# First expert layer of a transformer block: 256 of its 448 input rows by Strassen's seven block products, with banks of PSUM seeded by other engines

## The chip, the cores and the metric

The kernel runs on one core of a Trainium2 chip. Its engines work side by side, each through its own list of instructions, and wait for each other by semaphores: TensorE (PE in the profile; its weight loads are PEld) multiplies matrices into PSUM, VectorE (DVE), ScalarE (ACT) and GpSimd (POOL) do the element-wise work, and SyncE (SP) issues most DMAs. PSUM has eight banks of 512 float32 columns for each of 128 partitions. The metric is the device time of one execution in microseconds; lower is better.

## What is computed

A parallel block on x of 2048 tokens and 448 features: x plus attention plus a mixture of experts, both on the normalised x.

```python
# A: 16 heads of 28; B: E = 8 experts, K = 8 of them chosen, so all
xn = _layernorm(x, axis=-1)
return x + _A_ref(xn, A_wqkv, A_wo) + _B_ref(xn, B_w_gate, B_w1, B_w2)
...
        for e in range(E):
            mask = (topk_idx == e)
            w = (gates * mask).sum(-1, keepdims=True)
            h = _silu(xf @ w1[e]) @ w2[e]
            out = out + w * h
```

Each expert has a first layer of 448 x 1792 and a second of 1792 x 448. Since eight of eight experts are chosen, every token goes through all of them.

## The kernel before

Precision comes from pairs of float16: each float32 operand is scaled and split in a high and a low part, and a product is three float16 matmuls (high x high, high x low, low x high). In SBUF `xs` holds the normalised x transposed, four row blocks of high and four of low (the fourth block has only 64 rows).

An expert's 1792 hidden columns are cut in 14 blocks of 128, and these in weight groups of 5, 5 and 4 (`GROUPS`), 24 groups in all. The tokens are cut in 4 chunks of 512. `hidden` (L970) makes one hidden block for one chunk: ten matmuls of 128 rows x 512 columns into one bank (L984) and one more on 64 rows only, the tail (L992). Tails use half of TensorE's rows, so two of them, on different row halves and into different banks, are issued side by side; tails of 4 or 6 blocks are gathered (`STAYS`). `silu` (L1022) takes the bank through a tanh (ScalarE), a product (VectorE), a high part (ScalarE) and a low part (GpSimd). `summed` (L1076) makes the second layer for 128 tokens, three matmuls of 448 columns for each block (L1091), which VectorE scales by the gate and adds to `acc` (L1103).

Weights are prepared a group ahead: `load_group` fetches them, `group_scales` finds a power of two, `split_w1` and `split_w2` (L508, L529) scale on ScalarE, take the high part there and the low part on GpSimd. Phase 0 normalises x, transposes it (by DMA for the later chunks) and makes queries, keys and values.

Attention runs beside the experts: a score tile of 128 x 1024 fills the two banks 0 and 1 (L1187), VectorE finds its maxima (L1191), ScalarE takes exponentials (L1207) and their high part (L1215), VectorE the low part (L1210); after transposes by DMA, TensorE weighs the values (L1262, L1269).

The order of all this is not written by hand. Every job is added to a `Plan` (L60) with its engine, an assumed duration, its buffers, what it reads and writes, and a due value `v`; `Plan.run` lists the jobs greedily, for each engine the job of lowest `v` among those that are ready and whose banks are free, and issues the instructions in that order. `Banks.find` (L264) gives out the banks: the pair 0 and 1 to scores, 4, 5, 6, 7, 3 and 2 to all else. On the chip each engine then runs its instructions in the order listed.

## Time and profile before

| | us |
|---|---|
| three runs | 2624.71, 2626.7, 2630.6 |
| median | 2626.7 |
| profiled execution | 2626.05 |
| its span, first to last instruction | 2624.0 |
| TensorE busy | 2610.8 (99%) |
| VectorE busy | 2222.0 (85%) |
| ScalarE busy | 1958.6 (75%) |
| GpSimd busy | 1175.0 (45%) |

An engine's busy time is the union of its instructions' records. A matmul's record runs past the time in which it keeps the next one waiting, so the price of a product is read from start to start in the timeline. Idle time of an engine counts only where the span depends on it.

### The profile page before, as it was taken

What the parts mean: (1) busy time and instruction counts of PE and PEld (TensorE: products, weight loads), DVE (VectorE), ACT (ScalarE), POOL (GpSimd) and SP (SyncE); (2) the same over time, 40 slices, a digit from 0 to 9 for tenths busy, and PEclk for the clock granted to TensorE, in tenths of its full rate; (3) what the DMA queues carried; (4) which work ended last, traced back from release to release, by engine and by line L of the source; (5) the groups of instructions that cost most, each with busy time, mean ns of one, the idle gap of its engine ahead of it and who ended that gap; (6) DMA issues with size and microseconds to landing.
All of it is one profiled execution on the core that took longest, in us unless ns stands there. A gap on an engine that the chain in (4) does not pass through costs nothing.

```text
span 2624.0 us, 46561 instructions
## 1 busy us (share of the span) xinstructions
PE 2610.8 (99%) x17215; PEld 1272.6 (48%) x17215; DVE 2222.0 (85%) x3326; ACT 1958.6 (75%) x2752; POOL 1175.0 (45%) x1081
## 2 busy tenths in 40 slices
PE   9999999999999999999999999999999999999999
...
PEclk9999999999999999999999999999999999999999
...
GB/s 263 167 136 165 157 161 180 161 149 169 162 179 153 167 163 175 166 160 161 173 155 175 150 160 172 157 154 167 162 170 171 149 168 162 146 177 154 156 105 61
DMA packets 1230355, 422.23 MB, mean 161 GB/s; under 512 B 1149232, under 2 KB 1194800, under 8 KB 1230128
## 3 DMA queue, kind: packets, MB, share of 16 engines
...
q14 instruction: 91, 0.75, 0.1%
q10 hardware_dynamic: 560, 0.02, 0.0%
...
## 4 chain that ended last, share of the span: by engine, by line
PE 89%; DVE 6%; ACT 3%; issue 2%; POOL 0%; DMA 0%; DVEq 0%; ACTq 0%; POOLq 0%
PE banks L1091 35%; PE banks L984 34%; PE banks L1187 8%; PE banks L1269 4%; PE banks L1262 2%; PE banks L992 2%; PE banks L835 2%; DVE pl L1210 2%; DVE banks L1191 2%; PE banks L1355 1%; ACT pf L1207 1%; PE banks L858 1%; ACT ph L1215 1%; DVE t L1030 1%; DVE acc L1103 0%
## 5 line engine op out<-in xcount | busy, mean ns | idle before, releaser
L984 PE MATMUL banks<-xs,w 128*128 128x512 f16 x4480 | 1033.6, 379 | 0.8 <-DVE acc L1103 0.5
L1091 PE MATMUL banks<-w,hh 128*128 128x448 f16 x3576 | 968.5, 352 | 1.7 <-DVE acc L1103 1.7
L1034 POOL TENSOR_TENSOR hl<-t,hh 128x512 f16<-128x512 f32 x448 | 601.3, 1352 | 785.9 <-ACT hh L1033 744.5
L1207 ACT ACTIVATE pf<-banks,mx 128x1024 f32<-128x1024 f32 x512 | 568.9, 1111 | 361.0 <-DVE mx L1191 320.5
L1210 DVE SCALAR_TENSOR_TENSOR pl<-pf,ph 128x1024 f16<-128x1024 f32 x512 | 716.9, 1402 | 84.0 <-ACT ph L1215 83.1
L1191 DVE CUSTOM_DVE_ANT_0 banks<-banks,zero,cneg 128x1024 f32<-128x1024 f32 x512 | 657.7, 1285 | 103.4 <-PE banks L1187 78.1
L984 PEld LDWEIGHTS <-w 128*128 128x128 f16 x4480 | 428.5, 97 | 547.3 <-issue 43.2
L1091 PE MATMUL banks<-w,hl 128*128 128x448 f16 x1788 | 629.9, 352 | 0.0
L1215 ACT ACTIVATE ph<-pf 128x1024 f16<-128x1024 f32 x512 | 537.8, 1052 | 5.1
L1091 PEld LDWEIGHTS <-hh 128*128 128x128 f16 x3576 | 347.5, 98 | 348.9 <-issue 8.4
L1027 ACT ACTIVATE t<-banks,the 128x512 f32<-128x512 f32 x448 | 299.4, 683 | 141.3 <-PE banks L992 83.2
L1030 DVE SCALAR_TENSOR_TENSOR t<-t,banks 128x512 f32<-128x512 f32 x448 | 297.2, 679 | 63.7 <-ACT t L1027 62.9
L1103 DVE SCALAR_TENSOR_TENSOR acc<-banks,gwe,acc 128x448 f32<-128x448 f32 x383 | 257.6, 676 | 74.7 <-PE banks L1091 73.5
L1187 PE MATMUL banks<-K,Q 112*128 112x512 f16 x1024 | 305.8, 379 | 3.5 <-ACT pf L1207 3.4
L1033 ACT ACTIVATE hh<-t 128x512 f16<-128x512 f32 x448 | 271.9, 623 | 27.7 <-PE banks L1091 20.5
L522 POOL TENSOR_TENSOR w<-r,w 128x512 f16<-128x512 f32 x112 | 145.8, 1303 | 249.6 <-ACT w L518 243.9
L1091 PEld LDWEIGHTS <-hl 128*128 128x128 f16 x1788 | 174.4, 98 | 163.9
L539 POOL TENSOR_TENSOR w<-r,w 128x448 f16<-128x448 f32 x112 | 127.1, 1137 | 137.3 <-ACT w L536 131.9
L1187 PEld LDWEIGHTS <-Q 112*128 112x128 f16 x1024 | 95.0, 98 | 108.7 <-issue 18.8
L1269 PEld LDWEIGHTS <-th 128*128 128x128 f16 x4096 | 119.2, 96 | 19.7 <-issue 6.4
L387 DVE TENSOR_REDUCE mx<-r 128x1 f32<-128x1280 f32 (+3 forms) x96 | 124.9, 1308 | 0.8 <-DMA r<-in_B_w_dram 0.8
L1269 PE MATMUL banks<-V,th 128*128 128x57 f16 x4096 | 122.3, 188 | 0.0
...
## 6 DMA issues: line engine op xcount, KB each, us to landing
K<-qk SPq DMA_DIRECT2D x512, 56.0 KB
...
Q<-qk SPq DMA_DIRECT2D x256, 28.0 KB
...
```

The costliest lines, as they stand in the source:

```text
L984: nc.tensor.matmul(z(), rows(w)[:, blk, :], xx, start=(i == 0 and not late), stop=(i == NTERM - 2 and late))
L1027: add("ACT", 686, lambda: nc.scalar.activation(t(), z(), AF.Tanh, scale=th_()[:, 0:1]), v, r=[z, th_], w=[t])
L1030: lambda: nc.vector.scalar_tensor_tensor(t(), t(), 1.0, z(), op0=ALU.add, op1=ALU.mult),
L1033: add("ACT", 621, lambda: nc.scalar.activation(hh(), t(), AF.Copy), v, r=[t], w=[hh])
L1034: add("POOL", 1159, lambda: nc.gpsimd.tensor_tensor(hl(), t(), hh(), ALU.subtract), v, r=[t, hh], w=[hl])
L1091: nc.tensor.matmul(y()[:, 0:D], a, wv, start=(i == 0 and u == 0), stop=(i == g - 1 and u == 2))
L1187: nc.tensor.matmul(b()[:, cs], q()[:, q0 : q0 + P], k()[:, cs], start=True, stop=True)
L1191: nc.vector.tensor_tensor_reduce(b(), b(), zero.to_broadcast([P, 2 * C]), cneg, HUGE, op0=ALU.add, op1=ALU.min, accum_out=m()[:, n, j : j ...
L1207: nc.scalar.activation(p(), s(), AF.Exp, bias=m()[:, n, j : j + 1], scale=-1.0)
L1210: nc.vector.scalar_tensor_tensor(l()[:, js], p(), P_SCALE, h()[:, js], op0=ALU.mult, op1=ALU.subtract)
L1215: add("ACT", 1060, lambda: nc.scalar.activation(h()[:, js], p(), AF.Copy, scale=P_SCALE), v, r=[p], w=[(h, j)])
L1269: nc.tensor.matmul(a()[:, n, kt // (NKT // 2), 0:n2], ths[n]()[:, kt], vb()[:, kt, 0:n2], start=(n == 0 and kt == 0), stop=(n == NB - 1 an ...
```

## The change

Two pairs of hidden blocks (0 and 1, 2 and 3 of a group) and one chunk now make a unit. Of the 448 input rows the first two blocks of 128 are taken as a 2 x 2 matrix of blocks: weights A with two row blocks and two hidden blocks, tokens B with two row blocks and two halves of 256 tokens. Strassen's scheme (in Winograd's form) makes the four output blocks from seven products of block sums instead of eight. Each is three float16 matmuls for each of the two pairs, 6 matmuls of 256 columns (`strassen`). Partial sums are shared by seeding: after A11 x B11 in bank b1, ScalarE copies b1 into b2; after S1 x T1 in b3, ScalarE copies b3 to the SBUF tile s5; after S2 x T2 is added in b1, VectorE writes b1 + s5 into b3; after S3 x T3, b1 + s5 into b4. TensorE then goes on accumulating in these banks. The other 192 rows are added as before, 8 matmuls of 256 columns for each output bank (`plain`) and half-height tails, two sets of four in a unit (`tails`). The fifth block of a group of 5 is made by `single`, eleven matmuls of 512 columns, the tail included at full price.

The sums of weights are made in `split_w1` on GpSimd in float32, then split; the sums of x (`sums_of_x`) in phase 0, on VectorE, ScalarE and GpSimd, and transposed by eight more DMAs. The eighth block of `xs` is gone and the sums have a tile `xt` of their own, which phase 0 uses before that for its staging. Banks have kinds (`KINDS`): b1 and b3 come from 3, 2, 7, 6; b2 and b4 from 4 and 5; second-layer sums from 6, 7, 3, 2, 1, 0. High and low parts of the hidden layer have 7 buffers in place of 8, now of 256 tokens for each of two blocks (`columns`); the split weights have three buffers (`wa`) of which a group takes two, and four (`wc`) of which it takes two or three.

The diff, cut to the first layer, the split weights, the sums of x and the loop:

```diff
-RW1, RW2, RH, RPP, RPF = 6, 6, 8, 2, 2
-STAYS = {5: (4, 6, 6, 4), 4: (4, 4, 4, 4)}
+RWA, RWC, RW2, RH, RHC, RT, RPP, RPF = 3, 4, 6, 7, 2, 2, 2, 2
...
+    KINDS = {"s": (0,), "z": (6, 7, 3, 2), "y": (6, 7, 3, 2, 1, 0), "f": (4, 5, 6, 7, 3, 2, 1, 0), "u": (3, 2, 7, 6), "e": (4, 5)}
...
+    W1S = {5: (4, 0, 2), 4: (0, 2)}
+
+    def split_w1(gi, i, v):
+        j = W1S[GROUPS[gi][2]][i]
+        pair = j < 4
+        js = range(j, j + 1 + pair)
...
+        if not pair:
+            add("ACT", 1372, lambda: (scale(), high()), v, r=[so], w=[*keys, (wc, 0)])
+            add("POOL", 1303, low, v, r=[*keys, (wc, 0)], w=[(wc, 1)])
...
+        def highs():
+            scale()
+            for a, h in plain(0):
+                nc.scalar.activation(h, a, AF.Copy)
+
+        def lows():
+            for (a, h), (_, l) in zip(plain(0), plain(1)):
+                nc.gpsimd.tensor_tensor(l, a, h, ALU.subtract)
+            a11, a21, a12, a22 = (r(k, k + 1, f, f + 1) for k in range(2) for f in range(2))
+            nc.gpsimd.tensor_tensor(a22, a21, a22, ALU.add)
+            nc.gpsimd.tensor_tensor(a21, a11, a21, ALU.subtract)
+            nc.gpsimd.tensor_tensor(a11, a22, a11, ALU.subtract)
+            nc.gpsimd.tensor_tensor(a12, a12, a11, ALU.subtract)
...
+        ab = [(r1, j, *k) for j in js for k in R1K[:1]]
+        add("ACT", 2050, highs, v, r=[so], w=[*keys, (wa, 0)])
+        add("POOL", 2500, lows, v, r=[(wa, 0)], w=[*ab, (wa, 1)], steps=6)
+        add("ACT", 630, high, v, r=keys, w=[(wc, 0)])
+        add("POOL", 1303, low, v, r=[*keys, (wc, 0)], w=[(wc, 1)])
+        add("ACT", 630, high_sums, v, r=ab, w=[(wa, 2)])
+        add("POOL", 1303, low_sums, v, r=[*ab, (wa, 2)], w=[(wa, 3)])
...
+            for j in range(2):
+                ns = c * TPC + j, c * TPC + 2 + j
...
+                def sums(xa=xa, ts=ts):
+                    b11, b21, b12, b22 = (xa()[:, i * P : (i + 1) * P] for i in range(4))
+                    t1, t2, t3, t4 = (ts()[:, i * P : (i + 1) * P] for i in range(4))
+                    nc.vector.tensor_tensor(t1, b12, b11, ALU.subtract)
+                    nc.vector.tensor_tensor(t2, b22, t1, ALU.subtract)
+                    nc.vector.tensor_tensor(t3, b22, b12, ALU.subtract)
+                    nc.vector.tensor_tensor(t4, b21, t2, ALU.subtract)
...
+        A11, A12, A22, S2, S3, S4, S1 = range(7)
...
+        def unit(gi, b, tick):
+            ws = [W1[gi, j] for j in (0, 2)]
+            name = f"{gi}_{b}"
+            b1, b3 = (ps_z(f"u{i}{name}", "u") for i in (1, 3))
+            b2, b4 = (ps_z(f"e{i}{name}", "e") for i in (2, 4))
+            s5 = buf("mp", [P, C], F32, f"s5{name}", tag="s5")
...
+            B11, B12, B21, B22 = ((xs[:, k, t[i]], xs[:, 4 + k, t[i]]) for k in range(2) for i in range(2))
+            T1, T2, T3, T4 = ((sums_x[:, i, tx], sums_x[:, 4 + i, tx]) for i in range(4))
+
+            def strassen(bank, slot, x, start=False):
+                def product():
+                    for q in range(2):
+                        h, l = (ws[q][0]()[:, a, slot * P : (slot + 1) * P] for a in range(2))
+                        for i, (w, xx) in enumerate(((h, x[0]), (h, x[1]), (l, x[0]))):
+                            nc.tensor.matmul(
+                                bank()[:, q * HC : (q + 1) * HC], w, xx,
+                                start=(start and q == 0 and i == 0), stop=True, skip_group_check=True,
+                            )
+                keys = [k for w, _ in ws for k in ((w, 0), (w, 1), (w, 2), (w, 3))]
...
+            def plain(bank, f, i):
+                def product():
+                    for q in range(2):
+                        w = ws[q][1]().rearrange("p (a k f c) -> p a k f c", a=2, k=2, f=2)[:, :, :, f]
+                        for ww, xx in (
+                            (w[:, 0, 0], xs[:, 2, t[i]]), (w[:, 0, 0], xs[:, 6, t[i]]), (w[:, 1, 0], xs[:, 2, t[i]]),
+                            (w[:, 0, 1], xs[:, 3, t[i]]),
+                        ):
+                            nc.tensor.matmul(
+                                bank()[:, q * HC : (q + 1) * HC], ww, xx, start=False, stop=True, skip_group_check=True,
+                            )
+                return product, 8 * H_NS, [*xkeys(b), *((w, a) for _, w in ws for a in range(2))]
+
+            def tails(banks_, f):
+                def product():
+                    for q in range(2):
+                        w = ws[q][1]().rearrange("p (a k f c) -> p a k f c", a=2, k=2, f=2)[:, 1, 1, f]
+                        for i, bank in enumerate(banks_):
+                            rs = slice(64 * i, 64 * (i + 1))
+                            nc.tensor.matmul(
+                                bank()[:, q * HC : (q + 1) * HC], w[rs], xs[rs, 3, t[i]],
+                                start=False, stop=True, skip_group_check=True,
+                            )
+                return product, 200 + 2 * H_NS, [*xkeys(b), *((w, a) for _, w in ws for a in range(2))]
...
+            done, v0 = lasty + lastz, at(spent[0]) - AHEAD
+            v = go([b1], strassen(b1, A11, B11, True))
+            add("ACT", 610, lambda: nc.scalar.activation(b2(), b1(), AF.Copy), v, r=[b1], w=[b2])
+            v = go([b3], strassen(b3, S1, T1, True))
+            add("ACT", 610, lambda: nc.scalar.activation(s5(), b3(), AF.Copy), v, r=[b3], w=[s5])
+            tick()
+            v = go([b1], strassen(b1, S2, T2))
+            add("DVE", 690, lambda: nc.vector.tensor_tensor(b3(), b1(), s5(), ALU.add), v, r=[b1, s5], w=[b3])
+            go([b2], strassen(b2, A12, B21), plain(b2, 0, 0))
+            tick()
+            v = go([b1], strassen(b1, S3, T3))
+            add("DVE", 690, lambda: nc.vector.tensor_tensor(b4(), b1(), s5(), ALU.add), v, r=[b1, s5], w=[b4])
+            go([b3], strassen(b3, S4, B22), plain(b3, 0, 1))
+            v = go([b2, b3], tails((b2, b3), 0))
+            silu(gi, b, (0, 0), b2, v)
+            silu(gi, b, (0, 1), b3, v)
+            tick()
+            go([b4], plain(b4, 1, 1))
+            go([b1], strassen(b1, A22, T4), plain(b1, 1, 0))
+            v = go([b1, b4], tails((b1, b4), 1))
+            silu(gi, b, (1, 0), b1, v)
+            silu(gi, b, (1, 1), b4, v)
+            tick()
+
+        def single(gi, b):
...
+                        nc.tensor.matmul(z(), rows[:, blk, :], xx, start=(i == 0), stop=(i == NTERM - 1))
...
+        def columns(gi, b, j, t):
+            if j == 4:
+                return HS[gi, b, 4], slice(t * P, (t + 1) * P)
+            c0 = j // 2 * HC + t % 2 * P
+            return HS[gi, b, (j % 2, t // 2)], slice(c0, c0 + P)
...
```

How the order moves. On TensorE, in weight group 10 (its weights are `w_10_...` before, `wa_...` and `wc_...` now). Before, the tails of four blocks of one chunk stand together between full products:

```order
L1187 MATMUL banks<-K_1_14154,Q_13788 128x512
L992 LDWEIGHTS w_10_1_12809
L992 MATMUL banks<-xs,w_10_1_12809 128x512
L992 LDWEIGHTS w_10_2_13013
L992 MATMUL banks<-xs,w_10_2_13013 128x512
L992 LDWEIGHTS w_10_3_13028
L992 MATMUL banks<-xs,w_10_3_13028 128x512
L992 LDWEIGHTS w_10_4_13051
L992 MATMUL banks<-xs,w_10_4_13051 128x512
L984 LDWEIGHTS w_10_3_13028
```

Now, four tails of one unit stand between a score product and the plain products into b4, whose first waits for VectorE:

```order
L1363 LDWEIGHTS Q_15023
L1363 MATMUL banks<-K_0_15041,Q_15023 128x512
L1132 LDWEIGHTS wc_0_14824
L1132 MATMUL banks<-xs,wc_0_14824 128x256
L1132 LDWEIGHTS wc_0_14824
L1132 MATMUL banks<-xs,wc_0_14824 128x256
L1132 LDWEIGHTS wc_2_14993
L1132 MATMUL banks<-xs,wc_2_14993 128x256
L1132 LDWEIGHTS wc_2_14993
L1132 MATMUL banks<-xs,wc_2_14993 128x256
L1121 LDWEIGHTS wc_0_14824
L1121 MATMUL banks<-xs,wc_0_14824 128x256 [waits DVE_49]
```

The tails have half the columns and come in two such sets a unit; the bank after them is one that VectorE has seeded.

On VectorE, which reads the banks, in group 10, around the silu products of chunk 3 (`t`) before:

```order
L1210 SCALAR_TENSOR_TENSOR pl_14302<-pf_0_14281,ph_14292 128x1024 [waits DMAHW7_49,Activation_49]
L1191 ISA banks,mx_14263<-banks,zero,cneg 128x1024 [waits PE_49]
L1191 ISA mx_14263 128x1
L1030 SCALAR_TENSOR_TENSOR t_1_3_14304<-t_1_3_14304,banks 128x512 [waits Activation_49]
L1030 SCALAR_TENSOR_TENSOR t_2_3_14311<-t_2_3_14311,banks 128x512 [waits Activation_49]
L1287 TENSOR_TENSOR u_14415<-banks,c_14235 128x456 [waits PE_49]
L1191 ISA banks,mx_14263<-banks,zero,cneg 128x1024 [waits PE_49,Activation_49]
L1191 ISA mx_14263 128x1
L1210 SCALAR_TENSOR_TENSOR pl_14302<-pf_1_14339,ph_14292 128x1024 [waits Activation_49]
L1030 SCALAR_TENSOR_TENSOR t_3_3_14452<-t_3_3_14452,banks 128x512 [waits Activation_49]
```

and now, in group 11's first unit, around the two additions (L1151, L1155), with the maximum over scores now on L1367, the eviction of the second layer on L1276 and the low half of the exponentials on L1386:

```order
L1276 SCALAR_TENSOR_TENSOR acc<-banks,gwe_14777,acc 128x448
L1151 TENSOR_TENSOR banks<-banks,s_0_16548 128x512 [waits PE_49,Activation_49]
L1386 SCALAR_TENSOR_TENSOR pl_16517<-pf_1_16520,ph_16494 128x1024 [waits Activation_49]
L1367 ISA banks,mx_16558<-banks,zero,cneg 128x1024 [waits PE_49,Activation_49]
L1367 ISA mx_16558 128x1
L1155 TENSOR_TENSOR banks<-banks,s_0_16548 128x512 [waits DVE_49,PE_49]
L1427 TENSOR_REDUCE top_16627<-mx_16092 128x4
L1428 TENSOR_TENSOR c_16626<-top_16627,mx_16092 128x8 [waits DVE_49]
L1386 SCALAR_TENSOR_TENSOR pl_16631<-pf_0_16582,ph_16594 128x1024 [waits DMAHW6_49,Activation_49]
L1205 SCALAR_TENSOR_TENSOR t_0_00_16643<-t_0_00_16643,banks 128x512 [waits Activation_49]
```

The additions stand among the same maxima, evictions and low halves as the silu products did, and TensorE waits for what they write.

On ScalarE, the last unit of group 10, the copies of b1 and b3 (L1146, L1148) among tanh (L1202), exponential (L1383) and high parts (L1391, L1208):

```order
L1202 ACTIVATE t_3_4_16240<-banks,the_14707 128x512 [waits PE_49,Pool_49]
L1383 ACTIVATE pf_0_16249<-banks,mx_16092 128x1024 [waits DVE_49]
L1146 ACTIVATE banks<-banks 128x512 [waits PE_49]
L1148 ACTIVATE s_3_16261<-banks 128x512 [waits PE_49]
L1391 ACTIVATE ph_16279<-pf_0_16249 128x1024 [waits DMAHW1_49,Activation_49]
L1453 ACTIVATE lt_16285<-banks 128x512 [waits DVE_49,PE_49]
L1208 ACTIVATE hh_3_4_16295<-t_3_4_16240 128x512
L1383 ACTIVATE pf_1_16326<-banks,mx_16092 128x1024 [waits DVE_49]
L1391 ACTIVATE ph_16279<-pf_1_16326 128x1024 [waits Activation_49]
L1383 ACTIVATE pf_0_16358<-banks,mx_16092 128x1024 [waits DVE_49]
L1202 ACTIVATE t_3_00_16373<-banks,the_14707 128x512 [waits PE_49,Pool_49]
L1202 ACTIVATE t_3_01_16378<-banks,the_14707 128x512 [waits PE_49,Pool_49]
```

Both copies stand behind an exponential, and the second right behind the first.

## Rows read from the trace of the kernel before

**Rows 1.** The page: span, then busy time of each engine (share of the span, instructions), then the granted TensorE clock in 40 slices of the span, in tenths, 9 standing for 0.9 or more.
```profile
span 2624.0 us, 46561 instructions
...
PE 2610.8 (99%) x17215; PEld 1272.6 (48%) x17215; DVE 2222.0 (85%) x3326; ACT 1958.6 (75%) x2752; POOL 1175.0 (45%) x1081
...
PEclk9999999999999999999999999999999999999999
```

**Rows 2.** Groups of instructions by line, engine and operation, shapes apart: line, engine, operation, out<-in, partitions x columns, xcount | busy us, mean ns of one | idle us of the engine just before them and who ended it. The first layer's full products and weight loads (L984) and its half-height tails (L992).
```profile
L984 PE MATMUL banks<-xs,w 128*128 128x512 f16 x4480 | 1033.6, 379 | 0.8 <-DVE acc L1103 0.5 <-DVE t L1030 0.2
...
L984 PEld LDWEIGHTS <-w 128*128 128x128 f16 x4480 | 428.5, 97 | 547.3 <-issue 43.2
...
L992 PE MATMUL banks<-xs,w 64*128 64x512 f16 x448 | 66.1, 380 | 0.5 <-ACT lt L1277 0.4
```

**Rows 3.** Timeline of TensorE in a stretch in the middle of the run: start us, us, engine, line, operation, out<-in, xcount. Equal neighbours are merged in one row.
```profile
1003.84 2.32 PE L984 MATMUL banks<-xs,w 128*128 128x512 f16 x10
1006.00 0.60 PE L1187 MATMUL banks<-K,Q 112*128 112x512 f16 x2
1006.43 2.32 PE L984 MATMUL banks<-xs,w 128*128 128x512 f16 x10
1008.69 0.61 PE L992 MATMUL banks<-xs,w 64*128 64x512 f16 x4
1009.23 1.25 PE L984 MATMUL banks<-xs,w 128*128 128x512 f16 x5
1010.32 0.60 PE L1187 MATMUL banks<-K,Q 112*128 112x512 f16 x2
```

**Rows 4.** The table of waits: who waited for whom, us in total, times, longest.
```profile
DVE banks L1191 <- PE banks L1187: 78.1, 72, 3.4
DVE acc L1103 <- PE banks L1091: 73.5, 75, 2.5
...
PE banks L1187 <- ACT pf L1207: 3.4, 5, 1.7
```

**Rows 5.** Busy time in one window, the stage in which experts and attention run together: window, us, then each engine's busy us (instructions), granted clock, DMA share, GB/s.
```profile
150.00:2500.00 2350.00, 2341.98 (x15748) 1143.75 (x15747) 2053.92 (x2992) 1815.16 (x2500) 1096.67 (x1000) 1.00 0.76 162
```

**Rows 6.** Timeline of TensorE at the very end, the closing tile's narrow second-layer products, columns as in rows 3.
```profile
2618.65 0.33 PE L1048 MATMUL banks<-w,hh 128*128 128x192 f16 x2
...
2619.64 0.29 PE L1048 MATMUL banks<-w,hh 128*128 128x144 f16 x2
...
2620.39 0.26 PE L1048 MATMUL banks<-w,hh 128*128 128x112 f16 x2
```

**Rows 7.** Groups by line as in rows 2: on VectorE the low half of a projection taken out of a bank (L844), the maximum over a score tile with its second instruction (L1191), the low half of the exponentials (L1210), a scaling of x (L730), a subtraction of two 128-column tiles (L942); on ScalarE the exponential (L1207), scaling and high half of a first-layer weight block (L517, L518), a copy out of a bank (L842), a 128-column copy (L762); on GpSimd the low half of a weight block (L522).
```profile
L1210 DVE SCALAR_TENSOR_TENSOR pl<-pf,ph 128x1024 f16<-128x1024 f32 x512 | 716.9, 1402 | 84.0 <-ACT ph L1215 83.1
L1191 DVE CUSTOM_DVE_ANT_0 banks<-banks,zero,cneg 128x1024 f32<-128x1024 f32 x512 | 657.7, 1285 | 103.4 <-PE banks L1187 78.1 <-ACT ph L1215 19.2 <-ACT r L535 1.5
...
L1207 ACT ACTIVATE pf<-banks,mx 128x1024 f32<-128x1024 f32 x512 | 568.9, 1111 | 361.0 <-DVE mx L1191 320.5 <-DVE rl L1305 16.2 <-DVE pl L1210 11.0
...
L522 POOL TENSOR_TENSOR w<-r,w 128x512 f16<-128x512 f32 x112 | 145.8, 1303 | 249.6 <-ACT w L518 243.9 <-DMA Q<-qk 3.5
...
L517 ACT ACTIVATE r<-r,scog 128x512 f32<-128x512 f32 x112 | 79.9, 713 | 9.7 <-DVE scog L422 9.6
...
L1191 DVE DVE_READ_ACCUMULATOR2_ANT mx<- 128x1 f32 x512 | 71.2, 139 | 0.0
L518 ACT ACTIVATE w<-r 128x512 f16<-128x512 f32 x112 | 70.5, 630 | 3.5
...
L844 DVE TENSOR_TENSOR ql<-banks,qh 128x512 f16<-128x512 f32 x28 | 19.1, 685 | 16.8 <-ACT qh L842 16.7
...
L842 ACT ACTIVATE qh<-banks 128x512 f16<-128x512 f32 x28 | 16.4, 589 | 23.2 <-PE banks L835 23.1
...
L730 DVE TENSOR_SCALAR xn<-acc,rstd,shift 128x448 f32<-128x448 f32 x12 | 7.1, 628 | 0.0
...
L762 ACT ACTIVATE xb<-xn 128x128 f16<-128x128 f32 x12 | 3.6, 300 | 0.0
...
L942 DVE TENSOR_TENSOR gw<-lg,gm 128x128 f32<-128x128 f32 x1 | 0.3, 294 | 0.0
```

**Rows 8.** Single lines: xcount, ns of one as min/median/max, first and last start us, shape. The low half of the exponentials, an addition of 112 columns on GpSimd, and the transposes of x as SP's queue issues them.
```profile
L1210 DVE SCALAR_TENSOR_TENSOR pl<-pf,ph x512: 1206/1225/4290, 134.8 to 2540.8; 128x1024 f16<-128x1024 f32 x171
...
L1299 POOL TENSOR_TENSOR u<-u x64: 384/390/1453, 182.7 to 2560.4; 128x112 f32<-128x112 f32 x64
...
L772 SPq DMA_TRANSPOSE xs<-xb x12: 1231/1234/2551, 32.1 to 66.9; - x12
```

**Rows 9.** Windows of the opening stage, columns as in rows 5.
```profile
75.00:100.00 25.00, 25.00 (x122) 11.80 (x121) 9.81 (x22) 18.23 (x36) 10.99 (x10) 1.00 0.63 179
100.00:150.00 50.00, 50.00 (x242) 22.55 (x241) 33.55 (x65) 29.91 (x45) 12.83 (x11) 1.00 0.55 147
```

**Rows 10.** Windows between 150 and 2500 us. First the sums over windows of 25 us, chosen by VectorE's busy share: 32 of them below 85%, 21 of 90 to 95%, 8 above 95%. Then a window of 100 us, of those from one full hundred to the next the one with the highest share of VectorE.
```profile
sum 800.00, PE 797.64 PEld 387.69 DVE 650.20 ACT 612.34 POOL 377.23; mean PE 24.93 PEld 12.12 DVE 20.32 ACT 19.14 POOL 11.79
...
sum 525.00, PE 522.37 PEld 256.29 DVE 486.56 ACT 403.22 POOL 223.44; mean PE 24.87 PEld 12.20 DVE 23.17 ACT 19.20 POOL 10.64
...
sum 200.00, PE 198.83 PEld 98.79 DVE 195.21 ACT 152.49 POOL 91.12; mean PE 24.85 PEld 12.35 DVE 24.40 ACT 19.06 POOL 11.39
...
1300.00:1400.00 100.00, 99.75 (x628) 47.49 (x627) 91.61 (x132) 80.59 (x112) 52.09 (x47) 1.00 0.77 173
```

325 lines of the change are left out of this document (182 added, 143 removed).

## The prediction

> **What bounds the kernel now.** I read the page first. TensorE is busy for 2610.8 of 2624.0 us, at the full granted clock in every slice; VectorE for 2222.0, ScalarE for 1958.6, GpSimd for 1175.0 [rows 1]. Busy time of matmuls hides short gaps, since a 512-column matmul is recorded for 379 ns [rows 2] while ten of them take 2.16 us from start to start [rows 3], so I went on to the waits. In the whole table TensorE has one row of note, score products waiting for an exponential: 3.4 us in five waits; VectorE, the other way round, waits 78.1 us for score products and 73.5 us for the second layer's sums [rows 4]. TensorE waits for almost nobody, others wait for it: the span is the sum of its streaming, and a change is worth the columns it takes off TensorE as long as the other engines keep up. How close they are shows in the stage from 150 to 2500 us: in 2350 us TensorE 2341.98 (8.0 idle), VectorE 2053.92 (87.4%), ScalarE 1815.16 (77.2%), GpSimd 1096.67 [rows 5].
>
> **What TensorE saves.** One product's price is a start-to-start time. 512 columns: 2.16 us / 10 = 0.216 us [rows 3]. There are no 256-column ones before, but narrower ones stand at the end: 12 of 192 columns in 2618.65 to 2619.64 us, 82.5 ns each, and 12 of 144 in 0.75 us, 62.5 ns each [rows 6]. That is 0.417 ns a column, so 256 columns take 82.5 + 64 x 0.417 = 109.2 ns, 1.2 ns over half of 0.216. The half-height tails run two at a time; a group of four costs 0.54 us to the next product, and the ten products ahead of it 2.26 instead of 2.16 [rows 3]: beyond two streams of 0.216 a group costs 0.10 + 0.11 = 0.21 us.
> Before: 4480 products [rows 2] x 0.216 = 967.7; 448 tails in pairs, 224 x 0.216 = 48.4; four tail groups for each of 24 weight groups, 96 x 0.21 = 20.2. Sum 1036.3 us.
> After: 24 groups x 4 chunks = 96 units of 7 x 6 + 4 x 8 = 74 products of 256 columns, 96 x 74 x 0.1092 = 775.8; eight half-height tails a unit, in pairs, 96 x 4 x 0.1092 = 41.9; but two tail groups a unit instead of one for four blocks, 192 x 0.21 = 40.3; and the fifth block of 16 groups by itself, 64 x 11 x 0.216 = 152.1. Sum 1010.1 us.
> The saving is 26.2 us, 1.0% of the span. Seven products for eight sound like more: only 256 of 448 rows take part, the tail groups double (20 us), and the single block loses its half-price tail (64 x 0.108 = 7 us). The other products stay.
>
> **What the change adds elsewhere.** (1) VectorE: two additions a unit, a bank plus an SBUF tile into a bank. Nearest row: a bank minus a tile into SBUF, 685 ns; writing a bank shows no surcharge, since the maximum that reads and writes 1024 columns of banks takes 1285 [rows 7]. 192 x 0.685 = 131.5 us. (2) ScalarE: two copies a unit out of a bank, 192 x 0.589 = 113 us [rows 7]. Splitting a pair of weight blocks cost 2 x (713 + 630) = 2.69 us there; now one scaling of 1024 columns (1.11 by the exponential's row), 128 and 256 columns (0.30, and about 0.42 between its neighbours), and 2 x 0.63: 3.09 us, so +0.4 x 48 = 19 us [rows 7]. (3) GpSimd: 2 x 1.303 a pair becomes 2 x 1.303 plus parts of 128 and 256 columns (0.39, about 0.66) and four sums of 128 (0.39 each by the median of a 112-column add [rows 8]): +2.6 us x 48 = 125 us, some 170 if each part of 128 takes the 0.6 mean of that row. All of it is beside TensorE; GpSimd goes to about 52% of its span and has the most room.
> (4) The sums of x, 8 sets: on VectorE two scalings (under 0.63 each) and four sums of 0.294 [rows 7], at most 2.4 us a set, 20 us, late in the opening stage, where VectorE has 9.81 of 25 and 33.55 of 50 us busy [rows 9]: 31 us of room, under TensorE's projection products. Their 8 transposes hold SP's queue 1.23 us each [rows 8], 9.9 us, and the first attention loads stand behind them. If that cover fails, 10 us at most; I take 0, since expert products stand ready. Attention's own pool opens only when phase 0's last buffers have been issued, so its VectorE work may start as much later, and 10 us less of 2324 would raise the share below by 0.4%.
> (5) VectorE also shares with GpSimd: the subtraction of two SBUF tiles has a median of 1225 ns, a longest of 4290 [rows 8] and a mean of 1402 [rows 7], so 512 x 0.177 = 91 us of its busy time is being held up. With 12% more GpSimd work, +11 us.
> The Trainium skill (SBUF — State Buffer, "Who interferes with whom") says that a VectorE instruction with both inputs in SBUF contends with a GpSimd instruction that reads SBUF. The trace agrees so far as that tail reaches; by this rule the new additions, with one input in PSUM, should not be held up.
>
> So VectorE's stage goes from 2053.9 to 2053.9 + 131.5 + 11 = 2196 us, in a stretch of 2350 - 26 = 2324: 94.5%; ScalarE to 1947, 84%. What does TensorE lose then? The same stage holds stretches of such density. In 32 windows with VectorE below 85% (mean 81.3%) TensorE idles 2.36 of 800 us (0.30%); in 21 of 90 to 95%, 2.63 of 525 (0.50%); in 8 above 95% (97.6%), 1.17 of 200 (0.58%) [rows 10]. At 94.5% I take 0.53% of 2324 = 12.3 us against 8.0 now: **+4.3 us**.
>
> **The waits inside a unit.** Banks now go from TensorE to another engine and back. A bank can be read 0.163 us after its last column (379 - 216); a copy is then 0.589. In 15 of 96 units only the six products of S1 (0.66 us) stand between A11 and S2, which refills the copied bank: at least 0.1 us lost each, 1.2 if an exponential (1.11) is just ahead: 1.5 to 18 us. For the additions the order puts at least 14 products, 1.53 us, between S3 and the bank that it seeds, and 12 to 14 between S2 and its users; the addition needs 0.163 + 0.685 = 0.85, so 0.5 to 0.7 is left for what is ahead of it in VectorE's queue, in the order shown a maximum of 1.28 + 0.14 [rows 7] or an eviction. In most units second-layer or score products widen these gaps. Bounds: 0 and two stalls of 0.8 us a unit, 154 us; nearest are the present waits of TensorE, a few us in all, because the written order fills with other ready products. I take **+4 us** for both kinds.
>
> Sum against the profiled execution (2626.05 us, 0.65 below the median of 2626.7): 2626.05 - 26.2 + 4.3 + 4 = 2608, 0.7% less. At the end nothing moves: the closing tile keeps its products.
>
> **Rivals.**
> *VectorE becomes the pace.* For: 94.5% is needed without break, and the best 100 us of the stage reach only 91.6% with TensorE already 0.25 short [rows 10]; scores and evictions hold banks until VectorE has read them, and the units keep four of eight. If 91.6% is all it sustains, the stage takes 2196 / 0.916 = 2397, 47 us longer: 2673, slower. It decides from 93.4% down (2196 / 2350). Against: 25 us windows of 97.6% with TensorE at 99.4%, and VectorE's idle time is mostly spent waiting for TensorE, so it need not be a limit. The Trainium skill (TensorEngine Tiling (Array Packing), "PSUM Bottleneck") warns that a faster TensorE leaves PSUM evacuation as the bottleneck; no row here shows VectorE setting the span yet. Chance 0.16: 0.02 faster, 0.05 same, 0.09 slower.
> *The hand-offs eat it.* Break-even is 26.2 us over 96 units, 0.27 us each. One full wait for a maximum in progress (1.28 us) a unit would be 123 us: 2723. For: VectorE runs its long instructions in the written order. Against: a TensorE with five noted waits now, though every bank of scores and sums already depends on the same engines. Chance 0.13: 0.02 faster, 0.05 same, 0.06 slower.
> *Half-width products cost more than half.* Each carries its own weight load, recorded at 97 ns [rows 2], close to the 109 of the stream. 3.5 ns on each of 96 x 78 would undo the gain. But 144-column products with such loads run at 62.5 ns [rows 6]. Chance 0.03, at or above 2626.
> *Forecast*: 0.68, nearly all faster (0.66; 0.02 same); its own range is 2597 to 2620.
>
> Faster by over 0.2% (below 2621.4) 0.70, within 0.2%, which is what a measurement here can tell from no change, 0.13, slower 0.17. Low end: the full 26 us and some of today's 8 idle gone, 2595. High end: a part of the VectorE case, 93% sustained (2361, +11), or 0.4 us a unit of hand-offs (+12), 2638.
>
> **What would show it.** Right: products of 256 columns 109 ns apart; 192 tail groups at 0.21 us over their stream; VectorE at 93 to 95% between 150 us and the end of attention; TensorE waits from the new additions and copies under 15 us in all; the granted clock at full. Wrong: the additions or ScalarE's copies high in TensorE's waits, VectorE at 97% or more with TensorE idle beside it, later score products, or a gap ahead of each group's first unit, where two sets of split weights must be ready at once with buffers for three.

## The result, and the profile after

The median is 2647.2 us (2645.7 to 2647.7) against 2626.0 for the kernel before in the same comparison: a ratio of 1.0077, interval 1.0059 to 1.0094. The change makes the kernel 0.8% slower; 2608 was forecast, with a range from 2595 to 2638. The profiled execution took 2647.7 us.

The page, for [rows 1]: span, TensorE's busy time, granted clock in 40 slices.

```profile
span 2645.9 us, 54809 instructions
...
PE 2596.9 (98%) x20863; PEld 1597.2 (60%) x20863; DVE 2350.1 (89%) x3567; ACT 2069.8 (78%) x2993; POOL 1356.0 (51%) x1377
...
PEclk9999999999999999999999999999999999999999
```

TensorE has fewer products to stream and is recorded busy 14 us less, but its span is 22 us longer: it stands. The table of waits, for [rows 4], where before had one row of 3.4 us:

```profile
PE banks L1105 <- ACT banks L1146: 14.3, 20, 1.9
PE banks L1363 <- ACT pf L1383: 10.4, 11, 1.8
PE banks L1105 <- DVE banks L1151: 9.9, 11, 1.8
```

TensorE now waits 14.3 us for ScalarE's copy of b1 to b2 (L1146), 9.9 us for VectorE's first addition (L1151), and three times as long as before for exponentials. The window of [rows 5]:

```profile
150.00:2500.00 2350.00, 2310.72 (x19010) 1433.68 (x19009) 2146.63 (x3148) 1905.43 (x2705) 1240.40 (x1247) 1.00 0.77 162
```

39.3 us of TensorE idle in place of 8.0, with VectorE at 91.3% and ScalarE at 81.1%.

A timeline of TensorE shows the products and one of the stands (columns as in [rows 3], with the idle time before a row and its releaser).

```profile
1801.44 0.82 PE L1105 MATMUL banks<-xs,wa 128*128 128x256 f16 x6
1802.09 0.82 PE L1105 MATMUL banks<-xt,wa 128*128 128x256 f16 x6
1802.75 0.60 PE L1363 MATMUL banks<-K,Q 112*128 112x512 f16 x2
1805.22 0.81 PE L1105 MATMUL banks<-xt,wa 128*128 128x256 f16 x6 [1.88 <-ACT banks L1146]
1805.87 0.82 PE L1105 MATMUL banks<-xs,wa 128*128 128x256 f16 x6
1806.53 1.04 PE L1121 MATMUL banks<-xs,wc 128*128 128x256 f16 x8
...
1808.99 1.04 PE L1121 MATMUL banks<-xs,wc 128*128 128x256 f16 x8
1809.96 0.39 PE L1132 MATMUL banks<-xs,wc 64*128 64x256 f16 x4
1810.29 0.60 PE L1363 MATMUL banks<-K,Q 112*128 112x512 f16 x2
```

Read the prices first. Six products of 256 columns take 0.65 us from start to start (1805.22 to 1805.87, 1805.87 to 1806.53 is 0.66), 109 ns each. The four tails and what they cost their neighbours: eight products that alone would be 0.87 us hold the next row for 0.97, and the tails themselves last 0.33 in place of two streams of 0.109; so 0.10 + 0.11 = 0.21. Both are the prediction's numbers. Then the stand: after A11 (1801.44, from `xs`) and S1 (1802.09, from `xt`) comes a score tile, and then TensorE is idle 1.88 us, because S2 (1805.22) may not add to b1 before ScalarE has copied it. ScalarE in the same time:

```profile
1801.45 1.11 ACT L1383 ACTIVATE pf<-banks,mx 128x1024 f32<-128x1024 f32 x1 [3.46 <-DVE rl L1481]
1802.86 0.30 ACT L1487 ACTIVATE ost<-os 128x112 f16<-128x112 f32 x1 [0.30 <-DVE os L1482]
1803.07 1.04 ACT L1391 ACTIVATE ph<-pf 128x1024 f16<-128x1024 f32 x1
1804.01 0.67 ACT L1202 ACTIVATE t<-banks,the 128x512 f32<-128x512 f32 x1
1804.58 0.59 ACT L1146 ACTIVATE banks<-banks 128x512 f32<-128x512 f32 x1
```

A11 is done near 1802.3. The copy (L1146) starts at 1804.58, behind an exponential, a small copy, the exponential's high part and a tanh, in the order as written; TensorE goes on 0.05 us after its end. The waits on copies are mostly of this kind. In the 96 units of the trace only 11 have nothing but S1 between A11 and S2, and these stand 6.3 us in all by the sum below; of the 29 that have a score tile there as well, 17 stand, for 11.2 us.

One sum serves for all that follows. For each product after 110 us I take the time from its start to the next start, less its own pace (columns x 0.417 ns + 2.4 ns, and 0.10 us where products that run side by side, the tails or the attention's L1438, begin or end); what is over 40 ns counts as a **stand**. Recorded idle time is smaller, since a product's record runs on while TensorE already stands. Before has 11.3 us of stands in 27 places, after 60.5 in 118: 19.9 on the copy, 15.0 on the exponentials, 12.8 on the first addition. Profiled time less stands is 2614.8 before and 2587.2 after. So TensorE's own stream fell by 27.6 us, and 49.2 us of stands came for it. (The expectations of w1 and w2 below put the standing at 76 us in after, 25 in before and 33 in w1; by this sum it is 60.5, 11.3 and 24.0.)

### The profile page after: what moved, and what is told of

Its sections match the earlier page's. It is cut to its first block, busy times and chain, and to the rows that moved or that the text cites. A ratio compares the mean times of both kernels' runs of the same rounds, so it can differ in the third digit from the quotient of the medians.

```text
span 2645.9 us, 54809 instructions
## 1 busy us (share of the span) xinstructions
PE 2596.9 (98%) x20863; PEld 1597.2 (60%) x20863; DVE 2350.1 (89%) x3567; ACT 2069.8 (78%) x2993; POOL 1356.0 (51%) x1377
## 4 chain that ended last, share of the span: by engine, by line
PE 54%; DVE 9%; ACT 3%; issue 2%; POOL 1%; DMA 1%; SPq 0%; DVEq 0%; POOLq 0%; ACTq 0%
PE banks L1265 22%; PE banks L1105 10%; PE banks L1121 8%; PE banks L1363 5%; PE banks L1177 3%; DVE banks L1367 3%; PE banks L1445 3%; DVE pl L1386 2%; PE banks L1438 2%; PE banks L1132 1%; DVE t L1205 1%; ACT pf L1383 1%; PE banks L1531 1%; DVE acc L1276 1%; ACT ph L1391 1%
## 5 line engine op out<-in xcount | busy, mean ns | idle before, releaser
L1209 POOL TENSOR_TENSOR hl<-t,hh 128x512 f16<-128x512 f32 x448 | 594.8, 1336 | 810.5 <-ACT hh L1208 753.6
L1383 ACT ACTIVATE pf<-banks,mx 128x1024 f32<-128x1024 f32 x512 | 568.4, 1110 | 287.3 <-DVE mx L1367 248.7
L1386 DVE SCALAR_TENSOR_TENSOR pl<-pf,ph 128x1024 f16<-128x1024 f32 x512 | 719.4, 1407 | 39.7 <-ACT ph L1391 38.7
L1367 DVE CUSTOM_DVE_ANT_0 banks<-banks,zero,cneg 128x1024 f32<-128x1024 f32 x512 | 658.1, 1285 | 69.5 <-PE banks L1363 56.2
L1391 ACT ACTIVATE ph<-pf 128x1024 f16<-128x1024 f32 x512 | 539.0, 1053 | 4.9
L1265 PEld LDWEIGHTS <-hh 128*128 128x128 f16 x3576 | 339.9, 98 | 335.9 <-issue 27.4
L1105 PEld LDWEIGHTS <-wa 128*128 128x128 f16 x4032 | 391.9, 98 | 141.6 <-issue 42.4
L1121 PE MATMUL banks<-xs,wc 128*128 128x256 f16 x3072 | 399.0, 273 | 0.0
L1202 ACT ACTIVATE t<-banks,the 128x512 f32<-128x512 f32 x448 | 298.4, 681 | 101.3 <-POOL hl L1209 50.1
L1105 PE MATMUL banks<-xt,wa 128*128 128x256 f16 x2304 | 313.2, 273 | 26.7 <-ACT banks L1146 14.3
L1121 PEld LDWEIGHTS <-wc 128*128 128x128 f16 x3072 | 294.3, 98 | 62.4 <-issue 15.8
L1363 PE MATMUL banks<-K,Q 112*128 112x512 f16 x1024 | 305.9, 380 | 11.2 <-ACT pf L1383 10.4
L1276 DVE SCALAR_TENSOR_TENSOR acc<-banks,gwe,acc 128x448 f32<-128x448 f32 x383 | 257.2, 677 | 59.0 <-PE banks L1265 58.1
L1208 ACT ACTIVATE hh<-t 128x512 f16<-128x512 f32 x448 | 273.9, 623 | 18.0 <-DVE t L1205 10.2
L1105 PE MATMUL banks<-xs,wa 128*128 128x256 f16 x1728 | 236.5, 273 | 0.0
L611 POOL TENSOR_TENSOR w<-r,w 128x448 f16<-128x448 f32 x112 | 136.5, 1228 | 76.2 <-ACT w L608 74.7
L1177 PE MATMUL banks<-xs,wc 128*128 128x512 f16 x704 | 164.9, 379 | 0.0
```

Of the source, the lines that this page charges most:

```text
L1105: nc.tensor.matmul(bank()[:, q * HC : (q + 1) * HC], w, xx, start=(start and q == 0 and i == 0), stop=True, skip_group_check=True,)
L1121: nc.tensor.matmul(bank()[:, q * HC : (q + 1) * HC], ww, xx, start=False, stop=True, skip_group_check=True,)
L1202: add("ACT", 686, lambda: nc.scalar.activation(t(), z(), AF.Tanh, scale=th_()[:, 0:1]), v, r=[z, th_], w=[t])
L1209: add("POOL", 1159, lambda: nc.gpsimd.tensor_tensor(hl(), t(), hh(), ALU.subtract), v, r=[t, hh], w=[hl])
L1265: nc.tensor.matmul(y()[:, 0:D], a, wv, start=(i == 0 and u == 0), stop=(i == g - 1 and u == 2))
L1276: lambda: nc.vector.scalar_tensor_tensor(acc[:, n, :], y()[:, 0:D], gb()[:, n : n + 1], acc[:, n, :], op0=ALU.mult, op1=ALU.add),
```

## The experiments

A reply, below, is a copy or addition on another engine that TensorE's next step in a unit needs. The expectations set four theories against each other. Density: the added work on VectorE and ScalarE makes every reply late. Hand-off: TensorE loses the whole of each wait for a reply. Half-width: the narrow products stream slower than reckoned. Written order: TensorE stands because nothing else is ready at that moment.

Ratios are to the kernel before, timed beside each. "Rest" is the profiled time less the stands; it tells whether the stands are all that differs.

| run | median us | ratio, interval | stands us | rest us |
|---|---|---|---|---|
| d1, before with the load at any time | 2690.0 | 1.0243, 1.0228 to 1.0258 | 57.7 | 2632.8 |
| d2, before with the load in its place | 2624.7 | 0.9996, 0.9987 to 1.0005 | 10.7 | 2613.9 |
| b1, before with the rule | 2621.8 | 0.9987, 0.9977 to 0.9996 | 8.3 | 2613.5 |
| o1, as o3 but additions with both inputs in SBUF | 2662.8 | 1.0140, 1.0125 to 1.0155 | 75.0 | 2586.8 |
| o2, copies free, order of after | 2643.1 | 1.0064, 1.0047 to 1.0081 | 57.7 | 2586.5 |
| o3, copies and additions free, order of after | 2638.5 | 1.0047, 1.0032 to 1.0063 | 52.7 | 2586.2 |
| x1, as o3, planned anew | 2650.5 | 1.0097, 1.0082 to 1.0112 | 63.5 | 2586.9 |
| e1, x1 with shifted attention | 2627.2 | 1.0008, 0.9998 to 1.0018 | 39.6 | 2587.5 |
| e2, after with shifted attention | 2644.4 | 1.0071, 1.0055 to 1.0087 | 59.1 | 2588.9 |
| w1, other order | 2611.2 | 0.9945, 0.9932 to 0.9957 | 24.0 | 2588.4 |
| a1, w1 without overlap | 2641.8 | 1.0060, 1.0043 to 1.0077 | 54.0 | 2587.6 |
| a2, after with overlap | 2619.2 | 0.9975, 0.9964 to 0.9985 | 32.6 | 2586.6 |
| w2, better order | 2601.8 | 0.9912, 0.9897 to 0.9927 | 14.9 | 2587.4 |
| a3, w2 with the rule | 2626.8 | 1.0005, 0.9995 to 1.0015 | 40.8 | 2587.2 |
| n1, w2 with copies and additions free | 2602.4 | 0.9915, 0.9898 to 0.9933 | 14.0 | 2588.0 |

Apart from d1, which lost time before 110 us, where this sum does not count, the rest is 2613.5 to 2614.8 for every kernel with eight products and 2586 to 2589 for every one with seven, in whatever order. What differs from run to run is the stands. In a few runs they hold something besides waits: products at the lower granted clock behind a long stand, which are over their pace though nothing holds them up. They make some 13 us of x1's stands, 9 of e2's, 7 of d1's, 3 to 5 of a1's, a3's and e1's, and under 2 of any other run's.

**Is it the load on the other engines?** My first try, d1, let the extra work start at any time.

```diff
+ if j < 2:   add("ACT", 610, <copy of a constant to scratch>, v)
+ elif j < 4: add("DVE", 690, <addition of constants to scratch>, v)
```

> The kernel before with the load of the change and none of its hand-offs: for every expert slice and quarter of the tokens two more ScalarE copies (512 columns) and two more VectorE additions (512 columns), 192 of each in all, which write a scratch tile that nobody reads; the order is planned anew with them in it. What the reference asks is still computed. Density theory: this alone gives the loss, 2640 us and more, with the score products (L992 in before) standing 10 us longer on the exponentials than the 4.8 us of before. Hand-off theory: the load alone costs under 8 us, 2627 to 2634 us, and TensorE's standing grows by no more than that. My term for it in the prediction was 4.3 us, 2630 us.

(The score products of before are L1187; L992 are the tails.) It took 2690.0 us, far above every theory's figure. The windows show why: the work stood ready from the start, ScalarE was busy 56.2 of the first 60 us (35.9 before) and TensorE 48.5 (57.7 before), and the setup came late. All of the work was done by 657 us. As a measure of the density of after it is void, but while the work lasts it shows a higher one:

```profile
300.00:700.00 400.00, 381.88 (x2527) 184.02 (x2524) 390.10 (x560) 294.89 (x404) 186.21 (x161) 0.99 0.71 154
```

VectorE is busy 97.5% of these 400 us, and TensorE idles 18.1 (1.7 in before). d2 ties the same work to the blocks:

```diff
+ if j < 2:   add("ACT", 610, lambda: nc.scalar.activation(idle_a, z(), AF.Copy), v, r=[z])
+ elif j < 4: add("DVE", 690, lambda: nc.vector.tensor_tensor(idle_d, z(), <0>, ALU.add), v, r=[z])
```

> The kernel before with the load of the change, this time in its place: behind the tanh's bank of every first to fourth hidden block, one more reader of that bank, a ScalarE copy (two blocks of the four) or a VectorE addition (the other two) of 512 columns into a scratch tile that nobody reads, 192 of each in all; TensorE waits for none of them except as the bank comes free 0.6 to 0.7 us later. What the reference asks is still computed. In the run d1 the same work could start at any time, was done in the first quarter of the span, and held up the attention's setup (TensorE busy 48.5 of the first 60 us against 57.7 in before), so it did not measure density. Density theory: 2640 us or more, as after. My prediction's term for density was 4.3 us: 2630 us. Written-order theory (the load fits as long as other products stand ready whenever TensorE waits for a reply): under 5 us, 2626 to 2631 us.

No difference from before. The window of d2:

```profile
150.00:2500.00 2350.00, 2345.05 (x15695) 1143.62 (x15694) 2129.92 (x3134) 1880.56 (x2660) 1102.37 (x995) 1.00 0.74 160
```

VectorE at 90.6% and ScalarE at 80.0%, near after's 91.3 and 81.1, and TensorE idle 5.0 us. At this density the added load of the two engines costs nothing; the density theory falls. (GpSimd's added work is not in d2, 1102 us in the window against 1240 in after; w2 below has it all and is faster than before.)

**Is it the replies themselves?** The next runs keep every engine's order of after and take away the readers of b1 that TensorE waits for. The copy of b3 into s5 and the writes into the second banks stay.

```diff
- lambda: nc.scalar.activation(b2(), b1(), AF.Copy)
+ lambda: nc.scalar.activation(b2(), <0>, AF.Copy)             # o1, o2, o3
- lambda: nc.vector.tensor_tensor(b3(), b1(), s5(), ALU.add)   # and b4
+ lambda: nc.vector.tensor_tensor(b3(), <0>, s5(), ALU.add)    # o1
+ lambda: nc.vector.tensor_tensor(b3(), b3(), s5(), ALU.add)   # o3
```

> The kernel after with the order of every engine kept row for row, but the ScalarE copy into the second bank and the two VectorE additions take a constant zero in place of the first bank, so TensorE waits for them only where it goes on in the bank that they fill, and no longer before its next product in the first bank. The part of the sum that they carried over is left out, so the hidden layer is another one. Hand-off theory (the loss is TensorE standing before its next product until ScalarE or VectorE has read the bank): the trace of after has 19.9 us of standing before L1105 on the copy (33 times) and 12.8 us on the additions (18 times); both go, so about 2647 - 33 = 2614 us. Density theory (131 us more VectorE work and 113 us more ScalarE work make every reply late, whoever asks): the work is all still there, so within 5 us of after, 2642 to 2650 us, with the standing moved to the score products and the second bank. Half-width theory (the narrow products and the half-height pairs stream slower than reckoned): unchanged, 2645 to 2649 us.

o1 was slower still: 2662.8 us (1.0140, 1.0125 to 1.0155). Its additions, with both inputs in SBUF, first as o1 has it, then as after has it, with one input in PSUM (min/median/max):

```profile
L1155 DVE TENSOR_TENSOR banks<-zero,s x96: 683/727/1651, 127.6 to 2632.7; 128x512 f32<-128x512 f32 x96
```

```profile
L1155 DVE TENSOR_TENSOR banks<-banks,s x96: 679/699/736, 127.4 to 2621.3; 128x512 f32<-128x512 f32 x96
```

Some now last 1.65 us, and VectorE is busy 46 us longer. The Trainium skill (SBUF — State Buffer, "Who interferes with whom") says that such an instruction contends with GpSimd's reads of SBUF; the pair of rows agrees. So o1 measured a new cost of its own making, and o3 repeats it without.

> As the run before it, but only the ScalarE copy takes the constant; the two additions read the first bank as in after. The carried-over part is left out of the second bank alone. Hand-off theory: the 19.9 us on the copy go and the 12.8 us on the additions stay: about 2627 us, and the run without either hand-off lies some 13 us below this one. Density theory: 2642 to 2650 us. If the copy is late only because TensorE came early (so that the time is lost a step later whatever it is that waits), the standing before the additions and before the score products grows by as much as the copy's goes, and the time is that of after.

> As o1 (order of after kept row for row, no reader of the first bank between its products), but each addition reads the PSUM bank that it writes in place of a constant in SBUF: in o1 the additions had both inputs in SBUF and took up to 1.67 us (median 0.73), and VectorE was busy 46 us longer than in after, a cost of its own. The carried-over part is again left out, so the hidden layer is another one. Hand-off theory: 2647 - 33 = 2614 us. Late-engine theory (in this order ScalarE and VectorE are behind at these places, so whatever TensorE reaches next waits as long; o2, which cut the copies alone, took 16 us off the waits at the copies and got 4 us): 2635 to 2645 us, with the standing before score products and second banks grown.

o2 got 4 us of the 19.9 that stood on the copy, and o3 8.7 of the 32.7 on copy and addition. The waits of o3:

```profile
PE banks L1363 <- ACT pf L1383: 16.4, 26, 1.9
PE banks L1105 <- DVE banks L1151: 4.6, 6, 1.2
PE banks L1105 <- ACT banks L1146: 4.1, 7, 1.2
```

The stands on copy and addition fell from 32.7 to 11.6 us (those left are first products in a bank that the reply fills), and those on exponentials grew from 15.0 to 25.3. In a fixed order a wait that is taken out mostly comes back at the next thing that is late. The hand-off theory, that each wait is worth its length, falls too.

**Is it the order?** w1 has all instructions, shapes and hand-offs of after.

```diff
-RWA, RWC, RW2, RH, RHC, RT, RPP, RPF = 3, 4, 6, 7, 2, 2, 2, 2
+RWA, RWC, RW2, RH, RHC, RT, RPP, RPF = 3, 3, 6, 7, 2, 3, 2, 2
...
-            done, v0 = lasty + lastz, at(spent[0]) - AHEAD
+            done, v0 = [], at(spent[0]) - AHEAD
-            v = go([b1], strassen(b1, A11, B11, True))
+            v = go([b1], strassen(b1, A11, B11, True), early=20, free=0)
...
+            v = go([b3], strassen(b3, S1, T1, True), early=60, free=0)
...
```

`done` is the rule: the last second-layer job and single block in the list, for which every product of a unit waits. The lines left out put the copy 20 and the additions 50 ahead, move the calls of `tick` (the steps of a unit at which second-layer groups are handed out), let the splitting of weights begin two of these steps later and, at the end of the file, change offsets between attention and experts.

> The kernel after with the same instructions, shapes and hand-offs, in another written order: a unit no longer has to wait until the second-layer products ahead of it are issued, its first two products are offered 20 and 60 us earlier so that their copies are made while TensorE has the unit before in hand, copies and additions are put ahead of other replies by 20 and 50 us, second-layer groups are handed out at other steps of the unit, and one buffer of the split weights is given up for a third of the tanh. Written-order theory (TensorE stands because at those moments nothing else is ready): the streams of after without standing are 2646 - 76 = 2570 us, and with as much standing as the kernel before has (25 us) that is a span of 2595, some 2597 us of time; 2595 to 2615 us. Density theory (VectorE busy 91% and ScalarE 81% of the middle stage make replies late in any order): 2635 to 2650 us. Hand-off theory (a reply takes so long that a unit can't be worked without a wait of 0.34 us): 2635 to 2650 us.

2611.2 us, 36 us under after and 0.55% under before. Which of the edits?

> The order of w1 (2611.2 us) with one thing taken back: a unit again waits until the second-layer products ahead of it are issued, its first two products are offered no earlier than the rest, and copies and additions are not put ahead. The other edits of w1 (third tanh buffer for one of the split weights, other steps for the second-layer groups, other offsets of the two streams of work) stay. If it is the overlap of a unit's start with the work ahead that takes TensorE's standing away: 2635 to 2650 us, with the standing before L1105 on the copy back at 10 us or more. If the order is only another draw among many and any edit moves it: anywhere from 2611 to 2650 us, with no reason for the standing to come back at the copy.

> The other way round: after with the overlap of w1 (a unit need not wait for the second-layer products, first two products offered 20 and 60 us earlier, copies and additions ahead by 20 and 50 us), the third tanh buffer and the other steps for the second-layer groups, but with all offsets between the attention's and the experts' work as in after. If the overlap carries w1's gain of 36 us, most of it is here too: 2612 to 2628 us. If the offsets carry it: 2635 us or more.

Both came out as the overlap has it: without it 2641.8, with it and the old offsets (and the old first step of the splitting) 2619.2. In a1 11.1 us of stands are back on the copy, 1.9 in w1. w2 is a shorter edit found along that line (the single block is free of the rule too). It also moves the offsets, `M_AT, A_AT, LEAD` from 60, 0, 130 to 57, 45, 70, which its expectation does not name.

> A shorter edit of the order than w1 and one that I think better: no unit and no single block waits for the second-layer products, the first two products of a unit are offered 20 and 10 us earlier, the additions are put ahead by 50 us, the third tanh buffer, second-layer groups handed out later in the unit. Instructions, shapes and hand-offs are those of after. By the written-order theory its floor is the span without standing of after and w1 (2646 - 76 = 2570 us; 2611 - 33 = 2578 us); with a third to a half of w1's 33 us of standing it comes to 2590 to 2605 us, under w1 and under both kernels of the case. Density theory: not under w1's 2611 us.

2601.8 us, 0.88% under before and 45 us under after; 14.9 us of stands. Its two longest rows of waits, and its window:

```profile
PE banks L1363 <- ACT pf L1383: 2.5, 4, 1.3
PE banks L1438 <- DMA tl<-pl: 2.3, 3, 1.4
```

```profile
150.00:2500.00 2350.00, 2340.51 (x19280) 1459.10 (x19279) 2162.87 (x3180) 1920.62 (x2741) 1263.55 (x1276) 1.00 0.76 163
```

No copy or addition is left at the top, and VectorE is at 92.0%, more than in after. TensorE's timeline about a unit's start shows what changed:

```profile
1169.31 0.82 PE L1105 MATMUL banks<-xs,wa 128*128 128x256 f16 x6
...
1172.80 0.60 PE L1363 MATMUL banks<-K,Q 112*128 112x512 f16 x2
1173.23 0.82 PE L1105 MATMUL banks<-xt,wa 128*128 128x256 f16 x6
...
1177.16 2.54 PE L1177 MATMUL banks<-xs,wc 128*128 128x512 f16 x11
1179.54 0.82 PE L1105 MATMUL banks<-xt,wa 128*128 128x256 f16 x6
```

A11 at 1169.31, S1 at 1173.23, S2 at 1179.54, with second-layer products, score tiles and the single block between. ScalarE's copy lies well inside:

```profile
1170.66 0.59 ACT L1146 ACTIVATE banks<-banks 128x512 f32<-128x512 f32 x1
```

Between the end of A11 and S2, after had S1 and a score tile, 1.1 us, for the reply to come; w2 has 9.6.

**The rule, the replies, or both?**

```diff
-            done, v0 = [], at(spent[0]) - AHEAD
+            done, v0 = lasty + lastz, at(spent[0]) - AHEAD       # w2 to a3; and after=lasty in single
```

> The order of w2 (2601.8 us) with the rule alone put back: a unit, and the single block of a five-slice group, again wait until the second-layer products ahead of them are issued; the earlier offer, the additions' 50 us, the third tanh buffer and the later hand-out stay. If the rule is what leaves TensorE without other work while a reply is out: a good part of the 45 us between after and w2 comes back, 2615 to 2640 us, with the standing before score products and L1105 up from 15 us to 30 or more. If any of the other edits did it: within 5 us of w2, 2597 to 2607 us.

The rule alone costs w2 25 us. The waits of a3:

```profile
PE banks L1363 <- ACT pf L1383: 8.8, 10, 2.7
PE banks L1105 <- ACT banks L1146: 6.4, 14, 0.8
PE banks L1105 <- DVE banks L1151: 3.7, 6, 1.0
```

> The kernel before with the rule of after: no hidden block starts until the second-layer products handed out ahead of it are issued. Its blocks need no reply between their products. If the rule alone costs the time, hand-offs or not: 2640 us or more. If it needs both, units that wait for replies inside and a rule that keeps other units out: 2622 to 2630 us, as before.

On before, the same rule costs nothing (it came out 4 us faster). Its blocks have no reply inside; that this is the reason is argued, since a block of eleven products differs from a unit in more than that. The converse, the rule without the first bank's replies, planned anew:

> The kernel after, rule and units as they are, with the first bank's readers taken away as in o3 (copy of a constant, additions that read the bank they write; the carried-over part is left out, so the hidden layer is another one), but with the order written anew for it: in o3 the order was still the one written for units that wait. If hand-offs need both (rule and replies), the standing should fall well below the 53 us of o3: 2590 to 2615 us. If the rule on a long serial unit is enough even without replies: 2630 to 2642 us.

This did not fit: 2650.5. TensorE's timeline at one of its stands, then GpSimd's, then three windows:

```profile
1047.20 2.54 PE L1177 MATMUL banks<-xs,wc 128*128 128x512 f16 x11
1050.24 0.59 PE L1363 MATMUL banks<-K,Q 112*128 112x512 f16 x2 [0.50 <-ACT pf L1383]
1053.88 1.01 PE L1363 MATMUL banks<-K,Q 112*128 112x512 f16 x2 [3.04 <-ACT pf L1383]
1058.21 1.01 PE L1363 MATMUL banks<-K,Q 112*128 112x512 f16 x2 [3.32 <-ACT pf L1383]
1059.01 1.49 PE L1105 MATMUL banks<-xs,wa 128*128 128x256 f16 x6
1060.29 2.55 PE L1105 MATMUL banks<-xt,wa 128*128 128x256 f16 x12
```

```profile
1056.56 2.13 POOL L590 TENSOR_TENSOR wa<-r,wa 128x512 f16<-128x512 f32 x1
1058.65 2.02 POOL L611 TENSOR_TENSOR w<-r,w 128x448 f16<-128x448 f32 x2
```

```profile
1030.00:1045.00 15.00, 15.00 (x158) 8.67 (x156) 14.14 (x30) 13.10 (x18) 6.29 (x10) 1.00 0.75 172
1045.00:1060.00 15.00, 8.13 (x35) 3.59 (x33) 12.90 (x18) 14.26 (x22) 14.27 (x16) 0.74 0.74 165
1060.00:1075.00 15.00, 14.80 (x115) 9.72 (x114) 13.18 (x19) 11.82 (x17) 7.19 (x5) 0.92 0.86 172
```

TensorE has three score tiles in 9 us, each waiting for an exponential. GpSimd splits the next weights until 1058.69 (L590), and the first products of the unit that uses them start at 1059.01, six of them in 1.28 us in place of 0.65 at the lower clock. The like happens near 1685, 2024 and 2330 us, 6 to 7 us each time. I read this as the experts' work running ahead of its weights, so that the order had only score tiles to offer; the trace itself shows TensorE waiting for exponentials alone. Two numbers hold the attention back against it:

```diff
-M_AT, A_AT, LEAD, END, LAND, TURN = 60.0, 0.0, 130.0, 2585.0, 3500, 4500
+M_AT, A_AT, LEAD, END, LAND, TURN = 60.0, 45.0, 80.0, 2585.0, 3500, 4500
```

> x1 (rule kept, the first bank's readers taken away, order written anew, 2650.5 us) with the attention's work set 45 us later against the experts' at the start and 50 us later at the end, two numbers of the order. In x1 the standing came in heaps of some 7 us at the start of an expert (1050 to 1059 us: three score products and nothing else, until GpSimd had the next slice's split weight ready 0.3 us before the first product that uses it). If x1 was slow because the experts' work ran ahead of its weights and not because of the rule: 2605 to 2625 us, with the heaps gone. If the rule with a serial unit is enough to cost the time: 2640 us or more.

> The kernel after, readers of the first bank and all, with the same two numbers (45 us later at the start, 50 us at the end). With e1 it gives the price of the replies under the rule: if the replies are the cause under the rule, this stays at 2635 to 2650 us while e1 falls to 2605 to 2625. If the two numbers alone mend it, 2605 to 2625 us here as well.

e1 is at 2627.2, 23 us under x1 and 2 us above its forecast; one heap of 11 us (1349 to 1371 us) and one of 4 are left. e2 stays at 2644.4. With the rule and these offsets the first bank's replies cost 17 us, some 5 of them as products at the lower clock. They are not all of it: e1, with the rule and without them, still has 39.6 us of stands, 17.6 of them on exponentials.

> w2 (2601.8 us) with its order kept row for row and the first bank's readers taken away as in o3 (the carried-over part is left out). If the replies themselves cost nothing once other work stands between a product and the one that needs its reply: 2599 to 2603 us, as w2, where the same cut in the order of after gave 8.7 us. If each unit still pays for them: 2590 us or less.

2602.4 against 2601.8: where other work stands between, the first bank's replies cost nothing that can be measured. Against e1, n1 lacks the rule and has w2's other edits, and its stands are 14.0 in place of 39.6. The replies left in the unit, the copy of b3 and the fills of the second banks, were not taken out in any run.

## Why the prediction was wrong

- **The stream: right.** 26.2 us were forecast, from 109.2 ns a product and 0.21 us a tail group; the rest of the profiled time fell by 27.6, and the timeline has both prices. "Half-width products cost more than half" is out.
- **Density, +4.3 us: a small step, and too much.** VectorE was put at 94.5% of the stage and reached 91.3%: the stage grew longer instead of shorter (the last low half of an exponential starts at 2559.9 us, 2540.8 in [rows 8]), and the 11 us of hold-up by GpSimd did not come (that instruction has a mean of 1407 ns, 1402 in [rows 7]). d2 puts the price of the load at nothing. "VectorE becomes the pace" is out at this density: w2 runs at 92.0% in 2601.8. At 97.5%, in d1, TensorE does stand.
- **"I take +4 us for both kinds": this step failed.** Stands grew by 49 us, 0.51 us a unit, where break-even was 0.27: 33 us on the copy and the first addition, 10 more at the score tiles. "The hand-offs eat it" is what happened, though its price was 123 us and the wait it named, behind VectorE's long instructions, was the smaller part: 12.8 us on the addition, 19.9 on ScalarE's copy.
- **Why the step failed.** I priced the case of S1 alone between A11 and S2 at 1.5 to 18 us, and it came to 6.3 (11 units in the trace; I had counted 15). I took a score product between them for cover, and lost 11.2 us there: in the stand shown the copy waited behind an exponential, a small copy, a high part and a tanh, where I had reckoned with one exponential at most, and TensorE lost 2.0 us by the sum of starts (my most was 1.2). Then I chose near 0 "because the written order fills with other ready products". That was read off the kernel before, whose ready products were other hidden blocks, free to run in any bank. The change takes just these away: a unit is one chain, and `done` keeps the next unit out until the second-layer products are issued. Cover that an order has today was counted as cover for a change that removes it.
- The gap ahead of a group's first unit, which I named as a sign of error, is seldom in after (2.0 us near 1067, at a score tile); x1 has it four times in full.

Not settled: of the 45 us between after and w2, 25 are the rule's (a3). The other 20 are spread over the earlier offer, the additions' 50 us, the third tanh buffer, the later hand-out of second-layer groups and the offsets (like ones alone got 3 us in e2), and no run parts these. The parts do not simply add: a1, which lacks w1's overlap but has its other edits, got 5 us. And no run takes the replies out of a3, so how the rule's 25 us divide between replies and the rest of the unit stays open.
